# Seven quarter products for the second product of blocks 2 and 3, and a new spread of the weight preparation

## The chip, the core and the metric

The kernel runs on one core of a Trainium2 chip. The metric is the device time of one execution in microseconds. Names of engines: PE is TensorE, DVE VectorE, ACT ScalarE, POOL GpSimd, SP the engine from whose queue the DMAs are issued.

## The reference

Windowed attention over 3072 tokens of width 512 (4 sequences of 768, 8 heads of 64), and behind it two layers, each of two matrix products with a gate between them:

```python
x = attention(q, k, v, mem_k, mem_v)        # chunks of 32, softmax over 64 keys
h = x @ moe_w_in                            # 3072x512 @ 512x2048
x = (h * np.clip(h + 3.0, 0.0, 6.0) / 6.0) @ moe_w_out
h = x @ moe2_w_in
out = np.maximum(0.01 * h, h) @ moe2_w_out  # 2048x512
```

Inputs and result are fp32.

## The kernel before

The tokens are cut into six blocks of 512 columns. A matrix product at the wanted precision is made of three passes of PE: an operand is split into a high part (ACT copies it, line 341) and a low part (DVE subtracts, line 344), and PE takes high x high, low x high and high x low. The weights come from DRAM as 64-bit numbers; `decode` (lines 388 to 419) makes fp32 of them with one ACT instruction and three of DVE (lines 396 to 408).

The first layer is w1i (first product), the gate, and w1o (second product); the second layer has w2i and w2o. A product can be made plainly (`hidden`, `output`) or, for two blocks at a time, by seven products of quarter blocks in place of eight (Strassen's scheme). `seven` (line 1301) does so for first products, `second` (line 1437) for second products. For this the quarter weights, their sums and differences (a11, a12, a22, s1 to s4) are prepared by `prepare`, `joined` and `whole` (line 1208: four DVE instructions of 256 columns for each pair of weight blocks) and kept in DRAM (`kept`, `parted`); `left` (line 1255) loads a group of four quarters again when its product comes, and splits it into two parts of 1024 columns (one ACT, one DVE instruction).

The pairs of blocks have numbers: p = -2 is blocks 2 and 3, p = -1 blocks 4 and 5 of the first layer, p = 0, 1, 2 the three pairs of the second layer. Blocks 0 and 1 of the first layer are plain, with the attention of the later blocks running among them. Before the change p = -2 has its first product by `seven` and its second product plainly, block 2 and then block 3: `waiting_parts` (line 1412) splits the gated values and loads the w1o weights again, `output` (line 1027) multiplies, 12 matmuls of 512 columns for each of 16 weight blocks and each of the two blocks. p = -1 and the second layer go by sevens in both products.

What sets the order: all work is written as tasks with a key (the place in PE's sequence at which it is wanted, in units of four matmuls) and a number of buffers of each kind. `schedule` (line 103) runs a model of the engines and hands each engine its instructions in the order in which the model takes them; on the chip each engine goes through its list in that order and waits on semaphores. PE's products form one sequence, `seq2` (line 366). Preparing weights is filler: `PLAN` (lines 52 to 54) has for each of the 32 preparations a place from which it may run and a place at which it is due; before its due place it stands behind other work, from there on ahead of it. All preparation goes through DVE, ACT and SP's queue, beside the operands that PE's next products need.

Of the kernel before, what the change touches and what calls it, by code (L numbers as in the profile page):

```python
# [45 lines left out]
BOTH = 4  # L46
# [6 lines left out]
PLAN += [(290 + 9 * k, "1o", k, 320 + 9 * k) for k in range(8)]  # L53
PLAN += [(150 + 12 * k, "2i", k, 430 + 10 * k) for k in range(8)] + [(250 + 12 * k, "2o", k, 520 + 6 * k) for k in range(8)]
# [201 lines left out]
def tile_attn_moe_moe2(ctx: ExitStack, tc: tile.TileContext, raw, w1i, w1o, w2i, w2o, out):  # L256
# [41 lines left out]
    later = dram.tile([NT // (2 * N) + 1, KF // 2, 128, N], F32, name="later")  # L298
# [728 lines left out]
    def output(lay, j, f, c0, n, at=0):  # L1027
# [5 lines left out]
        if begin:  # L1033
            ybuf[lay, j] = [Buf(t) for t in ("hhyy" if j > 2 else "yyyy")]
# [248 lines left out]
    held, xs, ts1, t3s, c_of, sevens = {}, {}, {}, {}, {}, []  # L1283
# [17 lines left out]
    def seven(p, i, n):  # L1301
# [33 lines left out]
        if p < -1:  # L1335
            sevens.append(k)

        def put(r, after):
            held["b", p, i] = add(lambda e: nc.sync.dma_start(out=later[p % (PAIRED + 1), i], in_=r.t), {"SP": dma(N * 512, 330.0)}, key, after=[after], uses=[r])
# [29 lines left out]
        elif n == 7:  # L1369
            x = xs[p, i]  # L1370
            if p < -1:
                t3s[p, i] = y = Buf("w")
                done[7] = add(lambda e: nc.vector.tensor_tensor(out=half_of(y, 1), in0=bank(ba), in1=ut.t[:, 0], op=ALU.add), low, key, after=[k, done[5]], allocs=[y], uses=[ut, ba])
                c_of[p, i, "22"] = bent(lambda: y.t[:, 1], done[7], u(0), [y, ut])
                return
            done[7] = plus(lambda: x.t[:, 1], from_(ba), u(0), key, [k, done[5], c_of[p, i, "11"]], uses=[ut, ba, x])
            c_of[p, i, "22"] = bent(lambda: x.t[:, 1], done[7], u(0), [x, ut])
        elif n == 3 and p < -1:
            y = t3s[p, i]
            q = plus(lambda: y.t[:, 0], from_(bc), u(1), key, [k, done[6]], uses=[ut, bc, y])  # L1380
            c_of[p, i, "12"] = bent(lambda: y.t[:, 0], q, u(1), [y, ut])
        elif n == 4 and p < -1:
            x = xs[p, i]
            c_of[p, i, "21"] = gated(lambda: x.t[:, 1], from_(ba), [k, done[7], c_of[p, i, "11"]], lambda: x.t[:, 1], [ba, x])
# [27 lines left out]
    def waiting_parts(j, f):  # L1412

        key = pos_y["1", j, f] - 10
        src, c = (xs, t3s)[j - 2][-2, f // 2], f % 2
        z = len(quse)
        g = Buf("g" if z % OPS < 2 else "w")
        ready = [c_of[-2, f // 2, f"{c + 1}{j - 1}"]]
        hi = add(lambda e: copy(e, make(g, ([128, 2, N], F32R))[:, 0], src.t[:, c]), {"ACT": act(N)}, key, after=ready + (quse[z - OPS:z - OPS + 1] if z >= OPS else [c_of[-2, KF // 2 - 2, "22"]]), allocs=[g], uses=[src])
        lo = add(lambda e: minus(e, g.t[:, 1], src.t[:, c], g.t[:, 0].bitcast(F32)), {"DVE": dve(N)}, key, after=[hi], uses=[src, g])  # L1420
        gbuf["1", j, f, 0], gtask["1", j, f, 0] = g, (hi, lo)
        if j > 2:
            return
        w = Buf("w")
        whole_ = f >= KF // 2
        before = pos_y["1", j, f] - SOON - (3 if whole_ else 0)
        gate = max((t for t in sevens if t.key <= before), key=lambda t: t.key) if before < pos_y["1", j, 0] else ylast[j, (before - pos_y["1", j, 0]) // 3]
        k = add(lambda e: nc.sync.dma_start(out=make(w)[:, 1].bitcast(F32) if whole_ else make(w).bitcast(F32), in_=floats[f] if whole_ else halves[f]), {"SP": dma(262144 if whole_ else 524288, 360.0)}, pos_y["1", j, f] - 20, after=[gate, stored["1o", f]], allocs=[w])
        wbuf["1o", f], wtask["1o", f] = w, (k, k)
        if whole_:  # L1430
            hi = add(lambda e: copy(e, w.t[:, 0], w.t[:, 1].bitcast(F32)), {"ACT": act(512)}, key, after=[k], uses=[w])
            lo = add(lambda e: minus(e, w.t[:, 1], w.t[:, 1].bitcast(F32), w.t[:, 0].bitcast(F32)), {"DVE": dve(512)}, key, after=[hi], uses=[w])
            wtask["1o", f] = hi, lo
# [180 lines left out]
    for kind, j, f, *n in seq2:  # L1614
# [71 lines left out]
```

## Time and profile before

| | us |
|---|---|
| median of 3 runs | 1043.12 (1042.47 to 1044.17) |
| the profiled execution | 1042.63 |
| its span, first to last instruction | 1040.9 |
| PE busy | 1030.1 |
| DVE busy | 855.1 |
| ACT busy | 692.6 |

A page of the profile gives busy times and a chain that is followed back from the last instruction to what released it. PE's busy time is modelled from its pipelined matmuls, so a high share alone does not say that PE runs at its best; the distance from one matmul's start to the next does. For DVE and ACT the time shown for one instruction overlaps with the next by about 0.1 us, so what an instruction takes from the engine is read from one start to the next where instructions follow each other without a gap. The stages of the kernel follow each other in time, so busy time is read by stage.

### The profile page before, as it was taken

How to read it: one execution, taken by the hardware profiler on the slowest of the kernel's cores; microseconds unless marked ns; L12 is line 12 of the kernel's file. 1: busy time of each engine (PE TensorE's matmuls, PEld its weight loads, DVE VectorE, ACT ScalarE, POOL GpSimd, SP SyncE). 2: the span in 40 equal slices, each digit the busy share in tenths (PEclk: the TensorE clock that was granted, in tenths of full speed). 3: DMA queues.
4: the chain of work that ended last, by engine and by line, in shares of the span. 5: the costliest groups of instructions: out<-in, count | busy, mean ns of one | idle time of the engine just before them, and what ended most of it. 6: DMA issues, size and time to landing. Idle time of an engine off the chain costs nothing.

```text
span 1040.9 us, 20153 instructions
## 1 busy us (share of the span) xinstructions
PE 1030.1 (99%) x7476; PEld 849.9 (82%) x7476; DVE 855.1 (82%) x1423; ACT 692.6 (67%) x1478; POOL 22.3 (2%) x30
## 2 busy tenths in 40 slices
PE   7999999999999999999999999999999999999998
PEld 4788988888888888888888888888888888888887
DVE  6896897578999887599999898999466998566775
ACT  4896776656888554576786576775565874666753
POOL 4010000000000000000000000000000000000000
PEclk9999999999999999999999999999999999999999
DMA  9889787887897989464638894456342564522451
GB/s 266 297 241 324 258 281 238 254 293 221 286 315 232 328 280 322 157 214 135 215 129 281 268 299 151 152 170 204 128 156 81 182 200 143 179 105 99 144 182 61
DMA packets 127315, 220.50 MB, mean 212 GB/s; under 512 B 12528, under 2 KB 76016, under 8 KB 127216
## 3 DMA queue, kind: packets, MB, share of 16 engines
q1 hardware_dynamic: 127216, 219.20, 63.1%
q8 instruction: 59, 0.97, 0.4%
q14 instruction: 40, 0.33, 0.1%
HBM read 156.24 MB, written 62.91 MB: 211 GB/s over the span
## 4 chain that ended last, share of the span: by engine, by line
PE 96%; DMA 1%; DVE 1%; ACT 1%; issue 0%; SPq 0%; ACTq 0%; DVEq 0%
PE y L1322 17%; PE y L1047 15%; PE y L1490 13%; PE h L1322 11%; PE h L1490 8%; PE hx L1490 8%; PE hx L1322 8%; PE h L998 8%; PE h L1047 2%; PE at L634 2%; DMA w<-in_raw 1%; PE at L544 1%; PE at L602 1%; PE ac L461 1%; ACT w L845 0%; PE at L622 0%
## 5 line engine op out<-in xcount | busy, mean ns | idle before, releaser
L344 DVE TENSOR_TENSOR w<-w 128x512 fp32r<-128x512 f32 (+2 forms) x407 | 333.4, 858 | 28.6 <-ACT w L341 28.2
L341 ACT CAST w<-w 128x512 fp32r<-128x512 f32 (+1 forms) x296 | 226.5, 799 | 16.6 <-DMA w<-floats 7.2
L1322 PE MATMUL y<-w 128*128 128x512 f32 x516 | 124.5, 390 | 0.0
L1047 PE MATMUL y<-g,w 128*128 128x512 f32 (+1 forms) x540 | 124.4, 374 | 0.0
L1322 PEld LDWEIGHTS y<-w 128*128 128x128 f32 x516 | 96.7, 188 | 19.9
L1047 PEld LDWEIGHTS y<-g,w 128*128 128x128 f32 x540 | 94.2, 189 | 17.3
L341 ACT CAST g<-w 128x512 fp32r<-128x512 f32 x80 | 49.7, 622 | 67.6 <-PE y L1490 22.3
L1490 PE MATMUL y<-w 128*128 128x512 f32 x384 | 90.3, 389 | 0.0
L1490 PEld LDWEIGHTS y<-w 128*128 128x128 f32 x384 | 72.1, 188 | 14.9
L1296 ACT ACTIVATE w<-w 128x512 f32<-128x512 f32 x72 | 45.2, 631 | 43.0 <-DVE w L1289 21.5
L344 DVE TENSOR_TENSOR g<-w,g 128x512 fp32r<-128x512 f32 x80 | 54.8, 694 | 14.6 <-ACT g L341 14.4
L998 PE MATMUL h<-xh,w 128*128 128x512 f32 (+1 forms) x288 | 66.0, 370 | 0.0
L1490 PE MATMUL h<-w 128*128 128x512 f32 x264 | 62.1, 389 | 0.0
L1490 PE MATMUL hx<-w 128*128 128x512 f32 x252 | 59.2, 389 | 0.0
L1322 PE MATMUL h<-xl,w 128*128 128x512 f32 x240 | 58.2, 390 | 0.0
L1490 PEld LDWEIGHTS h<-w 128*128 128x128 f32 x264 | 49.6, 188 | 10.2
L998 PEld LDWEIGHTS h<-xh,w 128*128 128x128 f32 x288 | 49.7, 189 | 8.9
L1490 PEld LDWEIGHTS hx<-w 128*128 128x128 f32 x252 | 47.3, 188 | 9.8
L1322 PEld LDWEIGHTS h<-xl,w 128*128 128x128 f32 x240 | 44.9, 188 | 9.3
L1322 PE MATMUL y<-xh,w 128*128 128x512 f32 x216 | 52.0, 390 | 0.0
L1367 DVE TENSOR_TENSOR w<-y,w 128x512 f32<-128x512 f32 x35 | 24.0, 691 | 29.7 <-PE y L1322 26.9
L1322 PEld LDWEIGHTS y<-xh,w 128*128 128x128 f32 x216 | 40.5, 188 | 8.4
(243 smaller groups left out, 1836.5 us busy)
## 6 DMA issues: line engine op xcount, KB each, us to landing
w<-kept2i SPq DMA_DIRECT2D x42, 512.0 KB
w<-kept2o SPq DMA_DIRECT2D x42, 512.0 KB
w<-kept1i SPq DMA_DIRECT2D x28, 512.0 KB
a<-in_raw SPq DMA_DIRECT2D x20, 448.0 KB
w<-in_w1i SPq DMA_DIRECT2D x16, 512.0 KB
w<-in_w1o SPq DMA_DIRECT2D x16, 512.0 KB
w<-in_w2i SPq DMA_DIRECT2D x16, 512.0 KB
w<-in_w2o SPq DMA_DIRECT2D x16, 512.0 KB
```

Of the source, the lines that this page charges most:

```text
L341: nc.scalar.copy(out, in_) if e == "ACT" else engine(e).tensor_copy(out=out, in_=in_)
L344: engine(e).tensor_tensor(out=out, in0=a, in1=b, op=ALU.subtract)
L461: nc.tensor.matmul(x, ident, ident.unsqueeze(1).to_broadcast([128, c, 128]), start=True, stop=True, skip_group_check=True)
L544: nc.tensor.matmul(ps.t[h * CHUNK:(h + 1) * CHUNK, par, i * W:(i + 1) * W], qk[h // 2].t[r, gp, (h % 2) * G + c * CHUNK:(h % 2) * G + (c + ...
L602: nc.tensor.transpose(pt.t[:, i // NC, (i % NC) * 128:(i % NC + 1) * 128], pview()[:, i * 128:(i + 1) * 128], ident)
L634: nc.tensor.matmul(pv.t[(h % 2) * D:(h % 2 + 1) * D, par, (h // 2) * 2 * G + i * CHUNK:(h // 2) * 2 * G + (i + 1) * CHUNK], v[h // 2].t[r, ...
L998: nc.tensor.matmul(h.t[:, o:o + n], w.t[:, 1 if p == 1 else 0, k * 128:(k + 1) * 128], x[:, k, c0:c0 + n], start=(p == 0 and k == 0 and o ...
L1047: nc.tensor.matmul(bank(banks[d])[:, c0:c0 + n], w.t[:, 1 if p == 1 else 0, d * 128:(d + 1) * 128], g.t[:, 1 if p == 2 else 0, at:at + n], ...
L1296: return add(lambda e: nc.scalar.activation(out=at(), in_=at(), func=AF.Prelu, alpha=0.01), {"ACT": act(N)}, key, after=[after], uses=uses)
L1322: nc.tensor.matmul(bank(to), wt(l, o)[:, kt * 128:(kt + 1) * 128].bitcast(F32R), operand(p, name, 1 if q == 2 else 0, kt).bitcast(F32R), s ...
L1367: done[2] = add(lambda e: nc.vector.tensor_tensor(out=half_of(x, 0), in0=bank(bb), in1=ut.t[:, 0], op=ALU.add), low, key, after=[k, done[1 ...
L1490: nc.tensor.matmul(bank(to[d]), wt(1 if q == 1 else 0, o)[:, d * 128:(d + 1) * 128].bitcast(F32R), g.t[:, 1 if q == 2 else 0], start=(fres ...
```

## The change

Blocks 2 and 3 now have their second product by `second` too, seven products of eight steps of six matmuls; `waiting_parts` and the branches of `seven` for a plain second product go. The groups of w1o's quarters are loaded and split for p = -2 as well as for p = -1. The preparation of w1o may start at place 100 instead of 290; `joined` reads eight of w1o's blocks back from DRAM for it. The preparation of w2i may start at 305 instead of 150, that of w2o at 375 instead of 250, and their due places move by up to 12. `BOTH = 0` puts all decodes for the second layer into one chain.

The diff, cut:

```diff
-BOTH = 4
+BOTH = 0
...
-PLAN += [(290 + 9 * k, "1o", k, 320 + 9 * k) for k in range(8)]
-PLAN += [(150 + 12 * k, "2i", k, 430 + 10 * k) for k in range(8)] + [(250 + 12 * k, "2o", k, 520 + 6 * k) for k in range(8)]
+PLAN += [(100 + 1 * k, "1o", k, 100 + 13 * k) for k in range(8)]
+PLAN += [(305 + 3 * k, "2i", k, 430 + 9 * k) for k in range(8)] + [(375 + 13 * k, "2o", k, 508 + 6 * k) for k in range(8)]
...
-                if p < 0 and i == 0 and n == 1:
-                    seq2.append(("y", 0 if p < -1 else 3, KF - 1))
-        if p < -1:
-            seq2 += [("y", j, f) for j in (2, 3) for f in range(KF)][:-1]
-            continue
+                if p < -1 and i == 0 and n == 1:
+                    seq2.append(("y", 0, KF - 1))
         seq2 += [("q", p, n, i) for n in ORDER for i in range(KF // 2)]
...
+        if which == "1o" and f < KF // 2:
+            w = Buf("w")
+            k = add(lambda e: nc.sync.dma_start(out=make(w).bitcast(F32), in_=halves[f]), {"SP": dma(524288, 330.0)}, key, after=[stored[which, f], *gate], allocs=[w], late=LATE)
+            k = add(lambda e: nc.vector.tensor_tensor(out=make(m, ([128, 512], F32)), in0=w.t[:, 0].bitcast(F32), in1=w.t[:, 1].bitcast(F32), op=ALU.add), {"DVE": dve(512)}, key, after=[k], allocs=[m], uses=[w], late=LATE)
+            return m, k
...
-    def waiting_parts(j, f):
...
-            qbanks[p] = {m: [Buf(t), Buf(t)] for m, t in zip(FRESH, (("h", "hx")[p % 2], "y", "y"))} | {"m": [Buf("w"), Buf("w"), Buf("st"), Buf("st")]}
+            qbanks[p] = {m: [Buf(t), Buf(t)] for m, t in zip(FRESH, ("y", "h", "y") if p < -1 else (("h", "hx")[p % 2], "y", "y"))} | {"m": [Buf("w"), Buf("w"), Buf("st"), Buf("st")]}
...
-    prepare_before(180)
+    prepare_before(999)
...
-                x_pair(j + 1, pos_p[j + 1, 0, 1] - 18, 8)
+                x_pair(j + 1, pos_p[j + 1, 0, 1] - (18 if j > -2 else 16), 8 if j > -2 else 12)
...
-            if j > 1:
-                waiting_parts(j, f)
             output("1", j, f, 0, N)
-            if j > 1:
-                quse.append(ylast[j, f])
-            if (j, f) == (2, KF - 1):
-                prepare_before(999)
```

Two stretches of the program show the move. Line numbers are each kernel's own: `seven`'s matmuls are line 1322 before and 1324 in the changed kernel, `second`'s 1490 and 1454, the additions and the gate behind a first product 1289, 1373, 1350 and 1291, 1377, 1349, the weight preparation 396 to 408, 1189, 1208 and 393 to 405, 1186, 1210. Names: y, h and hx are PSUM banks, w and g operands in SBUF, at the attention's bank, mx its row maxima and sums, xh, xl and a the operands of a pair of blocks, wm, st and ys the weight preparation.

PE at the end of the first product of blocks 2 and 3, before:

```order
L1322 MATMUL h<-w 128x512 x12
L1047 MATMUL y<-g,w 128x512 x12
L602 MATMUL at<-ident,a 128x128 x6
L1047 MATMUL y<-g,w 128x512 x12
L634 MATMUL at<-a 64x32 x48
L1047 MATMUL y<-w 128x512 x48
L1047 MATMUL y<-g,w 128x512 x24
```

and in the changed kernel:

```order
L1324 MATMUL h<-xl,w 128x512 x12
L1324 MATMUL y<-w 128x512 x12
L1324 MATMUL h<-w 128x512 x12
L1454 MATMUL y<-g,w 128x512 x2
L599 MATMUL at<-ident,a 128x128 x6
L1454 MATMUL y<-g,w 128x512 x8
L631 MATMUL at<-a 64x32 x48
L1454 MATMUL y<-g,w 128x512 x2
L1454 MATMUL y<-w 128x512 x24
L1454 MATMUL y<-g,w 128x512 x12
```

The plain product's groups of 48 and 24 (line 1047) are gone; groups of `second` stand there, with the last attention units among them.

DVE at that place, before:

```order
L1373 TENSOR_TENSOR w<-h,w 128x512
L1189 TENSOR_TENSOR st<-w 128x512
L1289 TENSOR_TENSOR w<-y,xh 128x512
L1350 SCALAR_TENSOR_TENSOR w<-w 128x512
L1289 TENSOR_TENSOR w<-y,w 128x512
L1189 TENSOR_TENSOR st<-w 128x512
L1208 TENSOR_TENSOR ys<-st 128x256
L593 TENSOR_SCALAR mx<-mx 128x12
L594 RECIPROCAL mx<-mx 128x12
```

and in the changed kernel, beginning with the addition from bank h:

```order
L1291 TENSOR_TENSOR w<-h,w 128x512
L1210 TENSOR_TENSOR ys<-ys,wm 128x256
L344 TENSOR_TENSOR w<-w 128x1024
L1377 TENSOR_TENSOR w<-y,xh 128x512
L1210 TENSOR_TENSOR ys<-wm 128x256
L590 TENSOR_SCALAR mx<-mx 128x12
L591 RECIPROCAL mx<-mx 128x12
L1377 TENSOR_TENSOR w<-y,w 128x512
L1349 SCALAR_TENSOR_TENSOR w<-xh,w 128x512
L1349 SCALAR_TENSOR_TENSOR w<-w 128x512
```

w1o's blocks (line 1189) are no longer joined here; splits of 1024 columns and the preparation that was behind them have moved up.

DVE where the second layer begins, before, with w2o's preparation (lines 400 to 408) behind the operands:

```order
L344 TENSOR_TENSOR xl<-a,xl 128x512
L1532 SCALAR_TENSOR_TENSOR ys<-y,w 128x512 x2
L344 TENSOR_TENSOR g<-w,g 128x512 x2
L344 TENSOR_TENSOR w<-a,w 128x512
L344 TENSOR_TENSOR w<-w 128x512
L404 SCALAR_TENSOR_TENSOR wm<-w,wm 128x512
L400 TENSOR_SCALAR wm<-wm 128x512
L344 TENSOR_TENSOR w<-w 128x1024
L344 TENSOR_TENSOR w<-w 128x512
L408 SCALAR_TENSOR_TENSOR wm<-w,wm 128x512
L404 SCALAR_TENSOR_TENSOR wm<-w,wm 128x512
L408 SCALAR_TENSOR_TENSOR wm<-w,wm 128x512
```

and in the changed kernel:

```order
L344 TENSOR_TENSOR a<-a 128x512
L401 SCALAR_TENSOR_TENSOR wm<-w,wm 128x512
L397 TENSOR_SCALAR wm<-wm 128x512
L405 SCALAR_TENSOR_TENSOR wm<-w,wm 128x512
L401 SCALAR_TENSOR_TENSOR wm<-w,wm 128x512
L344 TENSOR_TENSOR xh<-w,xh 128x512
L405 SCALAR_TENSOR_TENSOR wm<-w,wm 128x512
L344 TENSOR_TENSOR a<-a,w 128x512
L344 TENSOR_TENSOR xl<-w,xl 128x512
L344 TENSOR_TENSOR xl<-a,xl 128x512
L344 TENSOR_TENSOR w<-a,w 128x512
L344 TENSOR_TENSOR w<-w 128x1024
```

Two decodes (lines 397 to 405) now stand between the operands of the second layer's first product (a, w<-a, xh, xl) and ahead of the split of 1024 columns that ends these rows.

## Rows read from the trace of the kernel before

**Rows 1.** The page's busy shares (engine, busy us, share, instructions) and its chain

```profile
PE 1030.1 (99%) x7476; PEld 849.9 (82%) x7476; DVE 855.1 (82%) x1423; ACT 692.6 (67%) x1478; POOL 22.3 (2%) x30
...
PE 96%; DMA 1%; DVE 1%; ACT 1%; issue 0%; SPq 0%; ACTq 0%; DVEq 0%
```

**Rows 2.** What PE waited for in all (us, times, longest), of seven rows

```profile
PE ac L461 <- ACT w L845: 2.0, 1, 2.0
...
PE at L602 <- DVE w L598: 1.2, 2, 0.9
```

**Rows 3.** The chain in order of time (start us, us, what), second products

```profile
504.23 10.88 PE hx L1490 x48
...
1026.47 10.89 PE h L1490 x48
```

**Rows 4.** Busy time of each engine by stage, the columns in the first line

```profile
core 0: us, PE busy (x) PEld busy (x) DVE busy (x) ACT busy (x) POOL busy (x), PEclk, DMA share, GB/s
246.80:341.00 94.20, 94.20 (x1051) 77.39 (x1051) 85.74 (x148) 77.78 (x218) 5.03 (x3) 1.00 0.82 264
341.00:424.10 83.10, 83.10 (x460) 68.87 (x459) 68.66 (x131) 40.41 (x73) 0.00 (x0) 1.00 0.88 297
424.10:504.20 80.10, 80.10 (x355) 66.42 (x354) 70.42 (x112) 53.91 (x84) 0.00 (x0) 1.00 0.55 181
504.20:580.40 76.20, 76.20 (x338) 63.17 (x337) 75.76 (x117) 52.85 (x86) 0.00 (x0) 1.00 0.61 212
580.40:656.50 76.10, 76.10 (x337) 63.07 (x337) 65.13 (x104) 52.62 (x84) 0.00 (x0) 1.00 0.66 218
656.50:732.70 76.20, 76.20 (x338) 63.17 (x337) 70.91 (x105) 52.26 (x86) 0.00 (x0) 1.00 0.53 180
```

**Rows 5.** The same view, the stretch in which DVE is full

```profile
440.00:575.00 135.00, 135.00 (x597) 111.91 (x596) 134.90 (x210) 96.23 (x152) 0.00 (x0) 1.00 0.58 195
```

**Rows 6.** DVE's instructions in order (start us, us, line, what): 1024, 512, 256 columns

```profile
513.91 1.23 DVE L344 TENSOR_TENSOR w<-w 128x1024 fp32r<-128x1024 f32 x1
515.05 0.70 DVE L344 TENSOR_TENSOR g<-w,g 128x512 fp32r<-128x512 f32 x1
515.65 0.70 DVE L344 TENSOR_TENSOR w<-w 128x512 fp32r<-128x512 f32 x1
...
519.26 1.23 DVE L344 TENSOR_TENSOR w<-w 128x1024 fp32r<-128x1024 f32 x1
...
453.54 0.43 DVE L1208 TENSOR_TENSOR ys<-st 128x256 f32<-128x256 f32 x1
453.87 0.43 DVE L1208 TENSOR_TENSOR ys<-st,ys 128x256 f32<-128x256 f32 x1
```

**Rows 7.** Groups of instructions by line (busy us, mean ns), 246.8 to 341 us

```profile
L561 DVE TENSOR_REDUCE mx<-at 128x12 f32<-128x768 f32 x4 | 3.8, 958 | 0.1
```

**Rows 8.** PE's instructions in order (start us, us, line, what) around attention units

```profile
251.47 1.17 PE L544 MATMUL at<-a 64*32 64x64 f32 x96
252.57 0.96 PE L1047 MATMUL y<-g,w 128*128 128x512 f32 x3
...
341.13 0.82 PE L602 MATMUL at<-ident,a 128*128 128x128 f32 x6
341.70 2.98 PE L1047 MATMUL y<-g,w 128*128 128x512 f32 x12
344.62 1.62 PE L634 MATMUL at<-a 64*64 64x32 f32 x96
346.17 6.19 PE L1047 MATMUL y<-w 128*128 128x512 f32 x26
```

**Rows 9.** Busy time and granted clock (PEclk) early in the trace

```profile
19.00:23.65 4.65, 2.68 (x18) 1.79 (x20) 4.22 (x12) 3.66 (x15) 2.86 (x3) 1.00 0.68 172
23.65:30.48 6.83, 6.83 (x109) 6.09 (x110) 5.41 (x10) 2.30 (x6) 2.59 (x4) 0.50 0.96 368
```

More of the change, by code (lines that the diff above doesn't have):

```diff
@@ L297, in tile_attn_moe_moe2 @@
     half = dram.tile([PLAIN, KD, 128, N], F32, name="half")
-    later = dram.tile([NT // (2 * N) + 1, KF // 2, 128, N], F32, name="later")
+    later = dram.tile([NT // (2 * N) + 2, KF // 2, 128, N], F32, name="later")
     attended = dram.tile([KD, 128, 4 * N], F32, name="attended")
@@ L1033, in output @@
         if begin:
-            ybuf[lay, j] = [Buf(t) for t in ("hhyy" if j > 2 else "yyyy")]
+            ybuf[lay, j] = [Buf(t) for t in "yyyy"]
         banks = ybuf[lay, j]
@@ L1104, in x_pair @@
         a, b = pair_of(p)
-        need = [yend["1", c] + [pk[p - 1, KF // 2 - 1, 4]] for c in (a, b)] if p >= 0 else [[*sent[a], *sent[b], *([ylast[3, 3]] if p == -1 else [])]] * 2
+        need = [yend["1", c] + [pk[p - 1, KF // 2 - 1, 4]] for c in (a, b)] if p >= 0 else [[*sent[a], *sent[b], *([pk[-2, KF // 2 - 1, 4]] if p == -1 else [])]] * 2
         homes = {"b11": "xh", "t2": "xl", "t3": "xl"} if p < -1 else {"b11": "xh", "t1": "xh", "t2": "xl", "t3": "xl"}
@@ L1281, in left @@
         return m, *ring[m]
-    held, xs, ts1, t3s, c_of, sevens = {}, {}, {}, {}, {}, []
+    held, xs, ts1, t3s, c_of = {}, {}, {}, {}, {}
     def plus(out, x, y, key, after, allocs=(), uses=()):
@@ L1334, in seven @@
         rlast[m] = [k]
-        if p < -1:
-            sevens.append(k)
         def put(r, after):
-            held["b", p, i] = add(lambda e: nc.sync.dma_start(out=later[p % (PAIRED + 1), i], in_=r.t), {"SP": dma(N * 512, 330.0)}, key, after=[after], uses=[r])
+            held["b", p, i] = add(lambda e: nc.sync.dma_start(out=later[p + 2, i], in_=r.t), {"SP": dma(N * 512, 330.0)}, key, after=[after], uses=[r])
         def u(c):
@@ L1370, in seven @@
             x = xs[p, i]
[L1371 to L1375, printed above, removed]
             done[7] = plus(lambda: x.t[:, 1], from_(ba), u(0), key, [k, done[5], c_of[p, i, "11"]], uses=[ut, ba, x])
             c_of[p, i, "22"] = bent(lambda: x.t[:, 1], done[7], u(0), [x, ut])
[L1378 to L1384, printed above, removed]
         elif n == 3:
@@ L1410, in made_as @@
         return b.t if b.t is not None else make(b, (shape, F32))
-    def waiting_parts(j, f):
[L1414 to L1433, printed above, removed]
     qbanks, quse, qops, qdone, qr = {}, [], {}, {}, {}
@@ L1454, in second @@
             r = Buf("w")
-            back = add(lambda e: nc.sync.dma_start(out=make(r, ([128, 2, N], F32)), in_=later[p % (PAIRED + 1), i:i + 2].rearrange("f p c -> p f c")), {"SP": dma(2 * N * 512, 360.0)}, pos - 20, after=[held["b", p, i], held["b", p, i + 1], *qops[p, 7, i]], allocs=[r])
+            back = add(lambda e: nc.sync.dma_start(out=make(r, ([128, 2, N], F32)), in_=later[p + 2, i:i + 2].rearrange("f p c -> p f c")), {"SP": dma(2 * N * 512, 360.0)}, pos - 20, after=[held["b", p, i], held["b", p, i + 1], *qops[p, 7, i]], allocs=[r])
             qr[p, i] = qr[p, i + 1] = r, back
@@ L1477, in second @@
         g = Buf("g" if z % OPS < 2 else "w")
-        hi = add(lambda e: copy(e, make(g, ([128, 2, N], F32R))[:, 0], src()), {"ACT": act(N)}, key, after=ready + (quse[z - OPS:z - OPS + 1] if z >= OPS else [c_of[p, KF // 2 - 1, "22"]]), allocs=[g], uses=[b])
+        hi = add(lambda e: copy(e, make(g, ([128, 2, N], F32R))[:, 0], src()), {"ACT": act(N)}, key, after=ready + (quse[z - OPS:z - OPS + 1] if z >= OPS else [c_of[p, KF // 2 - 2, "22"]]), allocs=[g], uses=[b])
         lo = add(lambda e: minus(e, g.t[:, 1], src(), g.t[:, 0].bitcast(F32)), {"DVE": dve(N)}, key, after=[hi], uses=[b, g])
@@ L1616, in tile_attn_moe_moe2 @@
             p, i, n = j, f, n[0]
-            if n == 1 and i == 0 and p == -1:
-                x_pair(p, pos_p[p, 0, 1] - 32, 12)
             seven(p, i, n)
```

## The prediction

> **What bounds the kernel now.** I read the page's busy shares and chain first, then who TensorE (PE) waits for, then the stages, then single instructions. On the page PE is busy for 1030.1 of 1040.9 us and the chain that ended last is PE for 96%; VectorE (DVE) has 82% and ScalarE (ACT) 67% [rows 1]. All that PE is shown to wait for lies in the attention and the warm-up ahead of it; no line of the two layers is in that list [rows 2]. From 504 us to the end the chain is nothing but groups of 48 matmuls in 10.88 us, 226.7 ns for each 128x512 matmul, the last group as fast as the first [rows 3]. So a matmul less is 0.2267 us less, as long as the other engines deliver.
>
> Whether they do is read by stage [rows 4]. The stages are: first product of blocks 2 and 3 (246.8 to 341), their second product, plain (to 424.1), first and second product of blocks 4 and 5 (to 504.2 and 580.4), then the second layer. DVE has 85.74 of 94.2 us, 68.66 of 83.1, 70.42 of 80.1 and 75.76 of 76.2. From 440 to 575 it is busy for 134.9 of 135 us [rows 5]: there DVE has no room, and PE is on time only because DVE had 14.4 us of room in the plain stage ahead of it. ACT has 26 us of room in 424 to 504. The average of 82% hides this.
>
> **The change, part by part.** The second product of blocks 2 and 3 was 32 steps of 12 matmuls (384); it becomes 7 x 8 steps of 6 (336). 48 matmuls x 0.2267 us = **10.88 us less on PE**. The profiled execution took 1042.63 us (span 1040.9), the median is 1043.12, so the sum stands 0.05% below the median's scale, which is nothing here. If PE stays the only limit: 1042.63 - 10.88 = 1031.75 us.
>
> What it costs is on DVE and ACT. The order of the changed kernel against the old one has on DVE 54 more instructions of 512 columns (low parts of 56 operands, the differences that seven products need and their joins, less the 40 low parts of the plain product and its weights, less 8 additions) and 12 more splits of 1024 columns (the quarter weights of w1o are now split twice, once per pair). An instruction of 512 columns holds DVE for 0.602 us, six of them from 515.65 to 519.26; one of 1024 for 1.14 (513.91 to 515.05); one of 256 for 0.33 [rows 6]. Together 54 x 0.602 + 12 x 1.14 = **46 us more on DVE**, against 10.9 us less time. ACT gets 27 more copies, 12 of them of 1024 columns, an estimate of 23 us if they take what DVE's take: I cost them at nothing; their cover is ACT's room, 42.7 us in the stage 341 to 424.1 alone [rows 4], and without it they would cost those 23. On SP's queue come 20 more DMAs, at nothing too: the DMA share is 0.88 in the plain stage, which loses its own reloads, and 0.55 to 0.61 in the two behind it [rows 4]; without that room weights would land late and PE would be seen to wait for DMAs.
>
> Where the 46 us fall decides. The weight preparation is spread anew: w1o's goes from behind the plain stage to ahead of it (it has to, its quarters are now needed 200 us earlier), w2i's goes from ahead of blocks 2 and 3 and among their first product to blocks 4 and 5, and w2o's follows it. So the stretch that was full stays full of preparation, and the stage that had 14.4 us of room gets the new operands.
>
> I price the stretch by one chain through the order, which leaves DVE no lead. It begins where DVE adds from a bank that PE has just filled (the addition from bank h that begins the changed kernel's rows of DVE in the first of the two stretches shown above; PE fills the bank 24 matmuls before the end of the first product of blocks 2 and 3), so DVE cannot be earlier there. It ends at the low part of a weight group of w2i (the last of DVE's rows in the second stretch) that PE wants for its 27th matmul of the second layer. DVE takes its rows in order. Between the two it has 321 instructions of 512 columns, 40 of 1024, 35 of 256 and 18 of 512 columns with one source, which take 0.33 as those of 256 do, and seven small ones of the attention, of which the reduction is the dear one at 0.96 us [rows 7]; an estimate of 1.4 us for the seven. 321 x 0.602 + 40 x 1.14 + 53 x 0.33 + 1.4 = 193.2 + 45.6 + 17.5 + 1.4 = **257.7 us**. PE has 24 + 3 x 336 + 27 = 1059 matmuls there, 240.0 us, and the end of two attention units: two transposes of 0.57 (341.13 to 341.70), two value products of 1.55 (344.62 to 346.17), one score product of 1.10 (251.47 to 252.57) [rows 8], 5.3 us. Together **245.3 us**. So PE must stand still for at least 257.7 - 245.3 = **12.4 us**, more than the 10.88 us it was spared. Counted the same way, the kernel before has no such chain: in its stretch 341 to 580.4 DVE has 214.8 us of work for 239.4 us [rows 4].
>
> Stage by stage the same count gives DVE 80.5 us in the new product (PE 81.5 with the attention), then 77.1 and 84.4 in the two products of blocks 4 and 5 (PE 76.2 each). So the end of the chain is where it hurts: on DVE, from 29 matmuls before the end of the second product of blocks 4 and 5 to that same group, stand 48 us of work for 39 us of PE. Weight preparation of w2i and w2o is 13.8 us of it (18 instructions at 0.33, 13 at 0.602); it is due there and goes ahead of operands that PE is about to want.
>
> On top come two terms that the chain leaves out. DVE's own waits inside it: at least as little as in 440 to 575 (0.1 in 135 us, so 0.2), at most what the stage of 246.8 to 341 loses (94.2 - 85.74 = 8.5 us). The chain's first third is of the kind of that stage, the rest of the full kind: I take 4. And the attention units, which now stand among the new product and wait behind more preparation: from 0 to 3, the list of waits having 1.2 us for two such [rows 2]; I take 1. Sum: 1042.63 - 10.88 + 12.4 + 4 + 1 = **1049.2 us**. After the chain PE is at its pace again: the same count gives DVE 77.5 and 75.4 us in the two products of the second layer's first pair, about PE's 76.2, and from there on what it was before.
>
> **Rivals.** *PE alone decides:* 1031.75 us, **faster**. For it: PE's 99%, no wait on DVE in the whole of the two layers, and 440 to 575, where a full DVE made PE wait for nothing. Against it: that is a full DVE, not an overfull one. The Trainium skill's "Perfetto Trace Analysis" (Identifying the Most-Contended Engine) says to find the engine with the highest occupancy and to optimize it first; by that the matmuls are the thing to save, and the sum would be 1031.75. The trace has DVE above PE's need in this stretch, and the same page (Optimization Strategy) allows that the most contended engine changes over time. Chance 0.07.
>
> *The chain is shorter than counted:* if DVE's waits are at their least and a part of the 256-column work overlaps, 1042.63 - 10.88 + 12.4 + 0.2 = 1044.4, about the time of before. Chance 0.10.
>
> *PE's clock falls in the new stalls:* early in the trace PE was busy 2.68 of 4.65 us up to 23.65, and then the granted clock was 0.50 (1.2 of 2.4 GHz) for 6.83 us [rows 9]. If stalls of the same size at the end of the chain bring it down once, PE does 3.4 us less in such a stretch: 1049.2 + 3.4 = 1052.6. "TensorE: Matmul & The Clock Gate" of the Trainium skill (HAM oscillation) has waits between groups of matmuls bring this about; the early rows agree, and no later row of before can show it, since PE never stops there. Chance 0.20.
>
> That the change does not do what it says is not open: the order has 4032 matmuls of 512 columns for 4080.
>
> **How the numbers follow.** The forecast, 0.63; the clock as well, 0.20; about equal, 0.10; faster, 0.07. The range begins at the floor of the chain, 1044.4, and ends with the dear ends of the two open terms and one fall of the clock: 1042.63 - 10.88 + 12.4 + 8.5 + 1 + 3.4 = 1057. A measurement can tell 0.2%, 2.1 us: faster is below 1041.0, slower above 1045.2. Faster 0.07, same 0.10, slower 0.83.
>
> **What would show it.** Right: the trace of the changed kernel has PE waiting for DVE's low parts (line 344's subtraction) for some 10 us in the 40 us around the start of the second layer, a few us more ahead of it, and DVE full from about 270 us to 640; PE's pace is 226.7 ns elsewhere. Wrong: DVE with room in that stretch (then the work was counted too high), a PE with no waits and a span near 1030, or waits that end with ACT or a DMA instead of DVE.

## The result and the profile after

The changed kernel took 1057.87 us (median of 4 runs, 1057.4 to 1058.98), the kernel before 1043.64 beside it: a ratio of 1.0128, 95% interval 1.0105 to 1.0152. It is slower, as forecast, but by 14 us and not by 6, and 0.9 us above the range. The profiled execution took 1058.05 us for a span of 1056.3, so it stands for the median.

The page's busy shares and its chain (engine, busy us, share, instructions), to be read beside [rows 1]:

```profile
PE 1025.3 (97%) x7428; PEld 839.0 (79%) x7428; DVE 897.6 (85%) x1489; ACT 710.8 (67%) x1505; POOL 22.9 (2%) x31
...
PE 77%; DVE 13%; DMA 5%; issue 3%; SPq 1%; ACT 1%; DVEq 0%; ACTq 0%
```

PE has 48 instructions less and DVE 66 more, as counted; the chain that was PE for 96% is PE for 77% and DVE for 13%. What PE waited for (us in all, times, longest); in [rows 2] no line of the two layers was named, now six of these seven are:

```profile
PE h L1324 <- DVE w L344: 5.1, 2, 5.0
PE hx L1454 <- DVE w L344: 3.4, 1, 3.4
PE y L1044 <- DVE g L344: 3.3, 1, 3.3
PE y L1454 <- DVE w L344: 2.1, 2, 1.4
PE ac L458 <- ACT w L842: 2.0, 1, 2.0
PE hx L1324 <- ACT xl L341: 1.6, 1, 1.6
...
PE y L1454 <- DVE g L344: 1.2, 2, 0.7
```

Busy time by stage, with the columns of [rows 4]. The stages are the new product (340 to 424), the two products of blocks 4 and 5 (to 508 and 588), and the two of the second layer's first pair:

```profile
246.00:340.00 94.00, 93.52 (x861) 75.53 (x860) 85.17 (x148) 71.55 (x187) 2.38 (x2) 1.00 0.91 298
340.00:424.00 84.00, 82.88 (x636) 67.52 (x635) 83.89 (x133) 61.62 (x127) 2.22 (x2) 1.00 0.76 251
424.00:508.00 84.00, 82.32 (x361) 67.21 (x360) 81.95 (x128) 59.03 (x93) 0.00 (x0) 1.00 0.58 192
508.00:588.00 80.00, 73.39 (x319) 59.15 (x318) 79.88 (x136) 51.31 (x84) 0.00 (x0) 1.00 0.81 269
588.00:664.00 76.00, 71.02 (x307) 58.30 (x306) 73.33 (x127) 53.67 (x89) 0.00 (x0) 0.98 0.85 279
664.00:740.00 76.00, 76.00 (x337) 62.72 (x336) 76.00 (x117) 54.37 (x89) 0.00 (x0) 1.00 0.60 198
```

DVE has next to no room from 340 to 588 (2.3 of 248 us), and PE stands still where it does not keep up, most of all in the 40 us ahead of 600. From 664 both are full and PE waits for nothing; the chain there is again groups of 48 matmuls in 10.88 us.

The worst of the waits, on PE (start us, us, line, what, and in brackets the idle time before it and what ended it), and what DVE did in that time:

```profile
593.34 0.61 PE L1324 MATMUL h<-xl,w 128*128 128x512 f32 x2
598.93 4.15 PE L1324 MATMUL h<-xl,w 128*128 128x512 f32 x10 [4.98 <-DVE w L344]
```

```profile
592.51 0.42 DVE L397 TENSOR_SCALAR wm<-wm 128x512 uint32<-128x512 uint32 x1
592.85 0.69 DVE L405 SCALAR_TENSOR_TENSOR wm<-w,wm 128x512 uint32<-128x512 uint32 x1
593.45 0.69 DVE L401 SCALAR_TENSOR_TENSOR wm<-w,wm 128x512 uint32<-128x512 uint32 x1
594.05 0.69 DVE L344 TENSOR_TENSOR xh<-w,xh 128x512 fp32r<-128x512 f32 x1
...
597.66 1.22 DVE L344 TENSOR_TENSOR w<-w 128x1024 fp32r<-128x1024 f32 x1
```

While PE waits, DVE decodes w2o (lines 397, 401 and 405), makes the low parts of the second layer's operands, and only then the low split of 1024 columns that PE wants: the group and the 27th matmul that the prediction named. It ends at 598.88.

**Where the time went.** The 1990th matmul from the end starts at 586.12 us in the trace before and at 598.94 in that after, 12.82 us later, although 48 matmuls (10.88 us) fewer lie ahead of it. So 23.7 us of PE's time were lost up to there, 1.9 behind it (1.7 of them by the clock, below) and 0.7 in the last stores: 23.7 + 1.9 + 0.7 - 10.88 = 15.4 = 1058.05 - 1042.63. Of the 23.7, the chain that the prediction counted makes 18.2: on DVE it ran from the addition out of bank h at 335.36 to 598.88, 263.5 us, for 245.3 us of PE's work. The other 5.5 lie ahead of it, 3.5 of them in one wait at 235 us. The last 2 are spread over the first 330 us in small pieces, and no run tells where they come from.

### The profile page after: what moved, and what is told of

It reads as the page before. It is cut to its first block, busy times and chain, and to the rows that moved or that the text cites. A ratio compares the mean times of both kernels' runs of the same rounds, so it can differ in the third digit from the quotient of the medians.

```text
span 1056.3 us, 20235 instructions
## 1 busy us (share of the span) xinstructions
PE 1025.3 (97%) x7428; PEld 839.0 (79%) x7428; DVE 897.6 (85%) x1489; ACT 710.8 (67%) x1505; POOL 22.9 (2%) x31
## 4 chain that ended last, share of the span: by engine, by line
PE 77%; DVE 13%; DMA 5%; issue 3%; SPq 1%; ACT 1%; DVEq 0%; ACTq 0%
PE y L1324 15%; PE y L1454 11%; PE h L1324 9%; PE h L1454 8%; PE h L995 8%; PE y L1044 8%; PE hx L1324 8%; DVE w L344 6%; PE hx L1454 4%; PE at L631 2%; DMA kept2i<-wm 1%; DMA w<-in_raw 1%; DVE g L344 1%; PE at L541 1%; DMA kept2i<-ys 1%
## 5 line engine op out<-in xcount | busy, mean ns | idle before, releaser
L344 DVE TENSOR_TENSOR w<-w 128x512 fp32r<-128x512 f32 (+2 forms) x453 | 365.7, 841 | 17.3 <-ACT w L341 17.2
L341 ACT CAST w<-w 128x512 fp32r<-128x512 f32 (+1 forms) x314 | 241.4, 806 | 10.2 <-DVE w L344 3.6
L1454 PE MATMUL y<-w 128*128 128x512 f32 x564 | 133.6, 390 | 2.1 <-DVE w L344 2.1
L1454 PEld LDWEIGHTS y<-w 128*128 128x128 f32 x564 | 105.5, 188 | 24.9 <-DVE w L344 2.9
L1324 PE MATMUL y<-w 128*128 128x512 f32 x516 | 124.5, 390 | 0.0
L1324 PEld LDWEIGHTS y<-w 128*128 128x128 f32 x516 | 96.6, 188 | 20.1
L1044 PE MATMUL y<-g,w 128*128 128x512 f32 (+1 forms) x432 | 96.8, 371 | 3.6 <-DVE g L344 3.3
L1044 PEld LDWEIGHTS y<-g,w 128*128 128x128 f32 x432 | 74.0, 189 | 17.3 <-DVE g L344 3.8
L1454 PE MATMUL y<-g,w 128*128 128x512 f32 x300 | 73.9, 392 | 1.2 <-DVE g L344 1.2
L1454 PE MATMUL h<-w 128*128 128x512 f32 x300 | 70.7, 389 | 0.0
L1454 PEld LDWEIGHTS y<-g,w 128*128 128x128 f32 x300 | 55.8, 188 | 14.2 <-DVE g L344 2.4
L344 DVE TENSOR_TENSOR g<-w,g 128x512 fp32r<-128x512 f32 x88 | 60.4, 693 | 7.5 <-ACT g L341 7.5
L1454 PEld LDWEIGHTS h<-w 128*128 128x128 f32 x300 | 56.2, 188 | 11.9 <-DVE w L344 0.3
L1454 PEld LDWEIGHTS hx<-w 128*128 128x128 f32 x252 | 47.2, 188 | 13.6 <-DVE w L344 3.8
```

Of the source, the lines that this page charges most:

```text
L341: nc.scalar.copy(out, in_) if e == "ACT" else engine(e).tensor_copy(out=out, in_=in_)
L344: engine(e).tensor_tensor(out=out, in0=a, in1=b, op=ALU.subtract)
L1044: nc.tensor.matmul(bank(banks[d])[:, c0:c0 + n], w.t[:, 1 if p == 1 else 0, d * 128:(d + 1) * 128], g.t[:, 1 if p == 2 else 0, at:at + n], ...
L1324: nc.tensor.matmul(bank(to), wt(l, o)[:, kt * 128:(kt + 1) * 128].bitcast(F32R), operand(p, name, 1 if q == 2 else 0, kt).bitcast(F32R), s ...
L1454: nc.tensor.matmul(bank(to[d]), wt(1 if q == 1 else 0, o)[:, d * 128:(d + 1) * 128].bitcast(F32R), g.t[:, 1 if q == 2 else 0], start=(fres ...
```

## The experiments

The theory: PE loses in each stretch between two ties (a DVE instruction that waits for PE, and a matmul that waits for a DVE instruction behind it) what DVE's work there exceeds PE's by, and the worst such stretch sets the loss. The rivals: the length of single hand-overs; late DMAs; the new operands alone; the moved preparation alone. "Excess" is DVE's work less PE's between two ties, counted through a kernel's order with the prices of the prediction. "Lost" is worked out from a trace: over all matmuls, the time to the next one's start less the median of that shape. Before, it is 47.5 us (mostly the attention and the start), after, 74.6. The length of a single wait is mostly given in this measure too; the idle time that a row shows in brackets is some 0.15 us shorter.

**1. More work inside the chain.** The sign step of w2i's decoding is done twice.

```
-            nc.vector.scalar_tensor_tensor(out=mu, in0=t.t[:, :, 1], scalar=0x80000000, in1=mu, ...)
+            for _ in range(2 if src is w2i else 1):
+                nc.vector.scalar_tensor_tensor(out=mu, in0=t.t[:, :, 1], scalar=0x80000000, in1=mu, ...)
```

> The changed kernel with the sign step of w2i's decoding done twice (the second time changes nothing): 16 more instructions of 512 columns on DVE, 14 of them inside the chain of 263.5 us that ends at 598.9 us, 2 ahead of it; the order of everything else is the same. Theory A, DVE's amount of work between the addition out of bank h and the low split of a w2i group decides, and every microsecond of it is a microsecond of PE's stall: 14 x 0.602 = 8.4 us, up to 9.6 with the two ahead, so 1057.9 + 8.4 to 9.6 = 1066.3 to 1067.5 us. Theory B, PE waits there for the length of one hand-over (bank, ACT, DVE, PE) and DVE has some room: at most 2 us, 1058 to 1060. Theory C, PE waits for weights whose DMAs are late: no change, 1058.

Measured: 1069.25 us (1066.32 to 1071.11), ratio to the kernel before 1.0222 [1.0181, 1.0262]. Its profiled execution took 1066.32, 8.3 us more than that of the changed kernel, and lost 83.0 us for 74.6: there the 8.4 us put in came out one for one, and the chain on DVE grew from 263.5 to 271.4 us. By the medians it is 11.4 us, 1.8 above the top of what was expected, so some executions lost more; what they lost it in is not shown. A hand-over's length (B, at most 1060) and late weights (C, 1058) are out as what sets the loss.

**2. Less work inside the chain.** The three DVE steps of w2i's and w2o's decoding on 64 of 512 columns.

```
+        cut = 64 if src is w2i or src is w2o else 512
-            mu = m.t.bitcast(U32)
+            mu = m.t[:, :cut].bitcast(U32)
```

> The changed kernel with the three DVE steps of w2i's and w2o's decoding done on 64 of the 512 columns, so the second layer's weights are wrong and all else, the order too, is as it was. 18 weight blocks are decoded inside the chain, at 0.33 + 2 x 0.602 us each; with an estimate of 0.1 to 0.13 for a short one that is about 21 us off DVE. Theory A: the chain falls from 263.5 to about 242 us, below PE's 245.3, so the 18.2 us of stall there go but for a few where DVE's instructions stand close together in front of PE, and the half clock after it goes too; the stall of 3.5 us at 235 us stays: 1038 to 1042 us. Theory B: the stall stays, 1055 to 1058. Theory C: 1058.

Measured: 1050.58 us (10 runs, 1048.8 to 1052.9), ratio 1.0058 [1.0038, 1.0077]. The sign was right, the size not: some 21 us of work off DVE gave back 7 and not 16 to 20. Two waits stayed around the second layer's start, of 2.4 and 2.7 us (572.7 and 588.7), and the clock fell after both; the wait at 235 us stayed too, as expected. DVE itself now stood idle for 13.6 us of the chain, for 2.3 in the changed kernel, and by the list of its waits most of that (10.5 us) was for ACT: much of what was taken off DVE went into waits for ACT. Counted with the short instructions, the whole chain has no excess left, but its last 28 us of PE's time still have 2.5 us. So the long chain was not the only one, and the last stretch had to be looked at by itself.

**3. The new places alone.** The kernel before, with w2i's and w2o's preparation where the change puts it.

```
-PLAN += [(150 + 12 * k, "2i", k, 430 + 10 * k) for k in range(8)] + [(250 + 12 * k, "2o", k, 520 + 6 * k) for k in range(8)]
+PLAN += [(305 + 3 * k, "2i", k, 430 + 9 * k) for k in range(8)] + [(375 + 13 * k, "2o", k, 508 + 6 * k) for k in range(8)]
```

> The kernel before, with its plain second product of blocks 2 and 3, and of the change only the new places of w2i's and w2o's preparation. Nothing is added to DVE; 35 us of it move from 150 to 340 us into the stretch of blocks 4 and 5. Theory A in its plain form (amount between two ties, whatever it consists of): counted through this order DVE has 13.9 us more than PE from 405 to 551 us of matmul time, and 2 to 5 us of its own waits on top: 1043.1 + 14 to 19 = 1057 to 1062 us, with the stall around the second layer's start. Rival D, it is the new operands of the seven products (46 us more on DVE) and not the moved preparation that makes the stall: 1043 to 1045.

Measured: 1060.84 us (1060.05 to 1062.14), ratio 1.0145 [1.0107, 1.0182]. Two lines of what its PE waited for, and two windows (columns as above):

```profile
PE hx L1490 <- DVE w L344: 5.0, 1, 5.0
PE h L1322 <- DVE w L344: 3.4, 1, 3.4
```

```profile
508.00:580.00 72.00, 70.08 (x302) 57.41 (x301) 71.01 (x120) 48.54 (x80) 0.00 (x0) 0.98 0.80 267
580.00:604.00 24.00, 15.35 (x56) 11.53 (x55) 24.00 (x44) 11.77 (x19) 0.00 (x0) 0.86 0.97 309
```

With no operand added, the moved preparation costs 16.5 us (1060.84 to 1044.31 beside it), at the same place and behind the same splits. Rival D is out: the new operands are not needed to make this loss.

**4. Cheaper new operands.** The 56 low parts of the new second product by a copy.

```
+        half_cost = p < -1
-        lo = add(lambda e: minus(e, g.t[:, 1], src(), g.t[:, 0].bitcast(F32)), ...)
+        lo = add(lambda e: copy(e, g.t[:, 1], g.t[:, 0].bitcast(F32)) if half_cost else minus(e, ...), ...)
```

> The changed kernel with the 56 low parts of the operands of the new second product of blocks 2 and 3 made by a copy of the high part (one source, an estimate of 0.33 us in place of 0.602), so that product is wrong and the order of all instructions is as it was. About 15 us of DVE's work go, all of it between 341 and 424 us, in the first third of the chain of 263.5 us. Theory A long (the sum over the whole chain decides, as predicted): 18.2 - 15 leaves about 3 us of stall, 1057.9 - 15 to 16.5 = 1041 to 1043 us. Theory A short (the last stretch of the chain decides by itself: counted through the order, from the additions that close the second product of blocks 4 and 5's second group to the same low split, DVE has 48.5 us of work for 38.5 us of PE, so that 10 of the 12.7 us of the whole chain's excess are made in its last 40 us): the stalls from 560 to 600 us stay, and only those at 342 to 350 and 428 us get smaller, 1054 to 1057 us. Which of the two is right also says whether the new operands or the moved preparation made the loss.

Measured: 1055.5 us (1054.21 to 1058.6), ratio 1.0121 [1.0102, 1.014], two windows of it, and below them the second one in the changed kernel:

```profile
340.00:424.00 84.00, 83.84 (x642) 68.94 (x643) 72.52 (x137) 62.52 (x129) 1.48 (x1) 1.00 0.76 263
560.00:600.00 40.00, 32.25 (x119) 24.43 (x118) 39.15 (x70) 19.79 (x33) 0.00 (x0) 0.87 0.93 307
```

```profile
560.00:600.00 40.00, 28.40 (x118) 21.53 (x117) 39.88 (x72) 19.46 (x33) 0.00 (x0) 0.99 0.95 318
```

DVE has 11.5 us of room in the new product, for 0.1 in the changed kernel, and the time falls by 2.4 us, less than the four executions differ among themselves. That room is of no use, because DVE cannot work ahead in it: by the trace it waits there 9.1 us for ACT's copies and 1.9 us for PE, and from 424 us on it is as full as before. From 560 to 600 us PE stands still for less time (it is busy 32.25 us for 28.40), but at a lower clock (0.87 for 0.99); DVE is full there in both kernels (39.15 and 39.88 us), and PE's slower matmuls take the place of waits: lost from 560 to 602 us are 13.5 for 14.8. "Short" is right: 10 of the 12.7 us of excess (12.4 in the prediction's count) are made in the last 38.5 us of PE's time, and counted again over the last 28 us it is 9.4.

**5. The old places.** The other part alone: the seven products, with the line of experiment 3 turned round (its "-" line in the changed kernel).

> The changed kernel with w2i's and w2o's preparation in the places that they had before, so the seven products of blocks 2 and 3 alone. Theory A short: counted through this order no stretch that ends at the second layer has an excess over 5 us, but one that ends in the new product does, 13.9 us between 275 and 312 us of PE's time (some 310 to 350 us in a trace), with 3.2 more ahead of it; so the stalls leave 560 to 600 us and come at 250 to 350 us, about as large: 1032.2 + 13.9 + 3.2 + 4 to 9 of DVE's own waits = 1053 to 1058 us. Rival D turned round (the moved preparation is the whole loss, the seven products cost nothing where the old places are kept): 1034 to 1040 us.

Measured: 1064.42 us (1063.45 to 1068.06), ratio 1.0208 [1.0189, 1.0228]; lost 80.8 us. Behind 376 us PE waits for nothing; the loss has left the start of the second layer for 200 to 376 us, as expected, and the time is 6 us above the top of what was expected. The row that was not foreseen, with PE's instructions in order:

```profile
356.45 1.12 PE L541 MATMUL at<-a 64*32 64x64 f32 x90 [0.17 <-ACT a L341]
367.80 1.54 PE L599 MATMUL at<-ident,a 128*128 128x128 f32 x6 [10.23 <-POOL a L595]
```

```profile
360.60:381.08 20.48, 10.87 (x116) 8.62 (x117) 18.39 (x33) 9.50 (x33) 1.56 (x1) 0.50 0.81 244
```

PE does the scores of an attention unit (line 541) until 357.57 and has nothing in its order between them and the unit's transposes (line 599), so it waits 10.2 us through the whole softmax. DVE is late by only 2.3 us of that (it takes the maximum at 359.8). The granted clock is 0.50 for 20.48 us, from within the wait on. In the changed kernel 46 matmuls (10.6 us) stand between the same two steps:

```profile
358.20 1.17 PE L541 MATMUL at<-a 64*32 64x64 f32 x96
...
369.89 0.81 PE L599 MATMUL at<-ident,a 128*128 128x128 f32 x6
```

So the order of the planner made this wait, and no count of DVE did. By an estimate from these rows the wait (10.2 us) and half of the 10.87 us that PE was busy at the half clock make 15.7 us; without them the time would be some 1049, below what the count gave. The run shows that the loss leaves the second layer's start with the old places, and that the seven products are not free there; the size that was counted it does not confirm.

**6. Two homes and an earlier start.** Pairs of w1o by turns in two sets of buffers, w2i from 261 + 9k.

```
-PLAN += [(100 + 1 * k, "1o", k, 100 + 13 * k) for k in range(8)]
+PLAN += [(100, "1o", k, 172 + 13 * k) for k in range(8)]
-PLAN += [(305 + 3 * k, "2i", k, 430 + 9 * k) ...
+PLAN += [(261 + 9 * k, "2i", k, 344 + k) ...
-            line = alone
-            parts = [joined(which, 2 * i + c, key, "st", line) for c in range(2)]
+            line = chains[1 - i % 2]
+            parts = [joined(which, 2 * i + c, key, ("st", "wm")[i % 2], line) for c in range(2)]
```

> The changed kernel with two edits to the preparation: pairs of w1o are prepared by turns in two sets of buffers (the second is idle there) so that one need not wait for the other's store, which the trace shows DVE doing ahead of the stall of 3.5 us at 235 us; and w2i's preparation starts earlier (261 + 9k, due at once). The count through the order has no excess left around 230 us and none in the last 40 us ahead of the second layer (-0.3), but 13.4 us for the stretch that ends 75 us before it. Theory A (any stretch between two ties, the worst one sets the loss): no stall at 235, the stall moves to 430 to 480 us, 13 to 16 us with DVE's waits: 1032.2 + 13.4 + 3 to 6 = 1049 to 1052 us. If only the last 40 us mattered: 1036 to 1040 us, faster than both kernels.

Measured: 1052.34 us (1051.45 to 1053.96), ratio 1.0091 [1.0075, 1.0108], 5.5 us better than the changed kernel. Windows around 235 us (the changed kernel's, then this one's), of the stretch where the count has the excess, and of the stretch ahead of the second layer:

```profile
230.00:240.00 10.00, 6.67 (x29) 5.20 (x29) 9.36 (x18) 4.95 (x10) 0.00 (x0) 1.00 0.94 306
```

```profile
230.00:240.00 10.00, 10.00 (x46) 8.29 (x45) 10.00 (x17) 6.24 (x14) 0.00 (x0) 1.00 1.03 410
424.00:508.00 84.00, 75.05 (x307) 60.42 (x306) 80.82 (x138) 52.31 (x82) 0.00 (x0) 0.92 0.71 244
508.00:588.00 80.00, 80.00 (x354) 66.27 (x353) 79.93 (x127) 54.71 (x89) 0.00 (x0) 1.00 0.65 215
```

The wait at 235 is gone, 508 to 588 us has none, and PE lost 14.6 us between 440 and 500 instead, where the count put 13.4. The two edits won 5.5 us, the wait at 235 among them; the rest of the loss they moved and did not remove.

**7. The same with light decoding.** Experiments 6 and 2 together.

> The two edits of the last experiment's kernel (two sets of buffers for w1o's preparation, w2i's preparation from 261 + 9k) and the decoding of w2i and w2o on 64 of 512 columns, so the second layer's weights are wrong: some 21 us less on DVE between 335 and 600 us. Counted through this order no stretch between two ties has an excess above 2.1 us. Theory A: the stalls from 430 to 480 us go but for 2 to 6 us of single short waits, none at 235 or 560 to 600, and the 10.88 us that PE was spared come through: 1031.75 + 2 to 6 = 1034 to 1038 us, faster than the kernel before. If the seven products cost PE something that no count of DVE shows (their operands' hand-overs, late DMAs): 1043 us or more.

Measured: 1042.99 us (10 runs, 1038.73 to 1046.34), ratio 0.9987 [0.9968, 1.0006]: no difference from the kernel before, and 5 to 9 us above what was expected. Its trace is of an execution of 1045.34, 2.3 us above the median; in it 340 to 360 us still lose 6.4 us and 440 to 480 5.7, for 1.0 and nothing before, in waits of 0.4 to 2.7 us each. So even with 21 us taken off DVE, nearly half of what the change adds, it only pays for itself: an excess near 2 us still brought some 11 us of loss, falls of the clock among it. A count of amounts is a floor; what stands above it is the order of single instructions on a full engine.

**8. GpSimd for the sums of quarter blocks.** 64 additions of 256 columns leave DVE.

```
-            ... nc.vector.tensor_tensor(out=part(name), ...), {"DVE": dve(256)}, key, ...
+            ... engine(e).tensor_tensor(out=part(name), ...), {"POOL": pool(256)} if which[0] == "2" else {"DVE": dve(256)}, key, ...
```

> The changed kernel with the four sums of quarter blocks of w2i and w2o (256 columns, 64 in all, 35 of them inside the chain) on GpSimd in place of DVE. Theory A: 35 x 0.33 = 11.6 us less in the chain, so its stall falls from 18.2 to about 7: 1057.9 - 11.6 = 1046, 1043 to 1049 with what the planner moves. Rival E, GpSimd's reading of the same memory slows DVE's instructions while it lasts (64 sums at an estimate of 0.7 us, from 1.31 us for its 512-column subtractions): DVE's own 512-column instructions get longer than 0.602 us on the mean, and half of the gain or all of it is lost, 1051 to 1058.

Measured: 1062.61 us (1061.1 to 1063.49), ratio 1.0159 [1.0121, 1.0197], 4.7 us worse than the changed kernel: rival E, and more than it gave. Two groups of the changed kernel from 335 to 664 us (line, engine, operation, tiles, shapes, count | busy us, mean ns | idle before), and the same of this one with GpSimd's:

```profile
L344 DVE TENSOR_TENSOR w<-w 128x512 fp32r<-128x512 f32 x74 | 48.6, 675 | 0.0
...
L1377 DVE TENSOR_TENSOR w<-y,w 128x512 f32<-128x512 f32 x15 | 10.2, 678 | 0.0
```

```profile
L344 DVE TENSOR_TENSOR w<-w 128x512 fp32r<-128x512 f32 x74 | 54.0, 752 | 0.0
...
L1377 DVE TENSOR_TENSOR w<-y,w 128x512 f32<-128x512 f32 x15 | 10.2, 685 | 0.2 <-PE y L1324 0.2
```

```profile
584.62 8.83 POOL L1210 TENSOR_TENSOR ys<-wm 128x256 f32<-128x256 f32 x1 [14.59 <-DMA spill<-ys]
```

DVE's subtractions of two tiles grow from 675 to 752 ns on the mean, those with one source in a bank of PE's (y) do not (678, 685); and one of GpSimd's sums, 0.73 us at its fastest, is shown for 8.83 us. "SBUF — State Buffer" of the Trainium skill (Who interferes with whom) says that a DVE instruction with two inputs in that memory contends with a GpSimd instruction that reads it; both rows agree.

Inside the chain the 11.6 us that left DVE made its work only 2.6 us shorter (258.6 us for 261.2), and its idle time grew from 2.3 to 7.3 us, which the rival had not named. The slow sums hold the buffer wm into which ACT scales the next raw block, and DVE waits for ACT, 6.4 us in two waits. The second of them, behind the sum of 8.83 us:

```profile
594.99 0.67 ACT L393 ACTIVATE wm<-w 128x512 f32<-128x512 f32 x1 [3.00 <-POOL ys L1210]
595.69 0.43 DVE L397 TENSOR_SCALAR wm<-wm 128x512 uint32<-128x512 uint32 x1 [2.84 <-ACT wm L393]
```

No version was found that beats the kernel before.

## Why the prediction was right and wrong

- **PE's 10.88 us: right.** The matmuls are fewer by 48, at the same pace wherever nothing is waited for.
- **DVE's 46 us: right in count** (66 instructions); the page's busy time grows by 897.6 - 855.1 = 42.5 us. That is another measure: an instruction by itself is busy for 0.69 us and takes 0.602 in a full row, so busy time does not test the 46.
- **ACT and SP at nothing: right but for one wait** of PE for ACT (1.6 us at 428 us); ACT has over 20 us of room in each stage, and only once did PE wait there. DVE waited 1.8 us for ACT in the chain as well, at 437 us, and ACT had itself waited 2.5 us for a store of w2i's quarters: that much the DMAs at nothing did cost.
- **The chain: right in kind, place and nearly in size.** Counted 257.7 us, measured 263.5, from the named addition to the named split. Its extra 5.8 us was the term "DVE's own waits", taken as 4, so the chain cost 18.2 us for 16.4. That 4 came near by luck, for it was taken from the room of other stages. Of the 5.8, 2.3 were idle (the wait for ACT just named, 1.8, is most of it), and 2.5 more are two instructions of 512 columns that took 1.87 and 1.96 us in place of 0.68, each while GpSimd multiplied for an attention unit. The first of them:

```profile
339.10 1.47 POOL L595 TENSOR_TENSOR a<-a,mx 128x768 f32<-128x768 f32 x1 [62.48 <-DMA kept1o<-ys]
339.25 1.87 DVE L1349 SCALAR_TENSOR_TENSOR w<-xh,w 128x512 f32<-128x512 f32 x1
```

  Every instruction of 512 columns that took over 1.2 us behind 200 us overlaps one of GpSimd, in the kernel before too. The prediction had no term for it.
- **The step that failed is the term for what lies ahead of the chain.** It was taken as 1, from 0 to 3, for attention units alone; it was 5.5, of which one wait of 3.5 us is explained. The diff moves w1o's preparation ahead of the last plain products of blocks 0 and 1, and the prediction said so, but priced DVE's work only from the first product of blocks 2 and 3 on. At 234 us DVE waits 0.64 us for a store that holds w1o's buffers and then has nine instructions, of which seven prepare w1o (joins at line 1186, sums at 1210, a low part), ahead of the low part of g that PE wants: 3.5 us. On DVE, and PE's row that ended behind it:

```profile
234.17 0.69 DVE L1186 TENSOR_TENSOR st<-w 128x512 f32<-128x512 f32 x1 [0.64 <-DMA kept1o<-st]
...
237.92 0.41 DVE L1210 TENSOR_TENSOR ys<-st,ys 128x256 f32<-128x256 f32 x1
238.26 0.68 DVE L344 TENSOR_TENSOR g<-r,g 128x512 fp32r<-128x512 f32 x1
```

```profile
238.99 0.73 PE L1044 MATMUL y<-g,w 128*128 128x512 f32 x2 [3.33 <-DVE g L344]
```

  DVE did have room shortly before (busy 9.40 of the 20 us from 200 to 220); by these rows it is the order of w1o's preparation and the operand that cost PE here, and not the amount. Experiment 6 took that store's hold away and moved w1o's due places, and the wait was gone; which of the two did it is not told. The other 2 us of the 5.5 stay open.
- **The clock: the rival came true by half,** beside the forecast and not in its place. Behind the wait of 5.0 us the granted clock was 0.50 from 599.17 to 602.58, 1.7 us of loss for the 3.4 given:

```profile
599.17:602.58 3.41, 3.41 (x9) 2.62 (x9) 3.28 (x8) 1.82 (x3) 0.00 (x0) 0.50 0.81 279
```

- **The sum:** 1042.63 - 10.88 + 18.2 + 5.5 + 1.9 + 0.7 = 1058.05. Against the forecast that is 1.8 more in the chain, 4.5 ahead of it, 1.9 behind it and 0.7 at the end. The range's upper end left the term ahead of the chain at 1; with 5.5 it would have held the measured time.
- **What would show it:** 12.4 us of waits for DVE's low parts from 560 to 600 us (some 10 were named), a few ahead, DVE full from 340 to 588 (not from 270) and again from 664. The reason was right in outline and was tested: work put into the chain came out one for one in the profiled execution (experiment 1). What the prediction didn't see is that the whole chain is not what decides, though it named the stretch: 48 us for 39 at its end are enough by themselves (experiments 3 and 4). So that 16.4 came near 18.2 does not show that the sum over the whole chain was the right sum: 15 us taken out of its first third gave back 2.4.
- **Readings of the prediction to put right:** that stretch of 39 us begins some 145 matmuls ahead of the end of the second product and not 29 (29 and 27 matmuls are 12.7 us). In the kernel before, w1o's preparation lay among the plain stage (its stores go out from 341 to 455 us) and not behind it, and its quarters are first loaded at 487 us there and at 322 in the changed kernel, 165 us earlier and not 200.
- **"PE alone decides", 1031.75:** out. Neither part of the change is free alone (experiments 3 and 5, the latter also without its one long wait, by the estimate there), and the best places that were tried left 8.9 us more than the kernel before (experiment 6).

What stays open: which of the single waits in experiment 7 come from the order that the planner wrote and which from the length of hand-overs; what experiment 5 would have taken with work between its scores and transposes, since no run has that; and the 2 us ahead of the chain.

## What to carry to other kernels

Where two engines are both near full, count the work of each between two points at which they are tied to one another, for short stretches as well as for long ones, and for every stretch that a moved step now crosses, the ones ahead of the change's own stage too. Room in a stage ahead is worth nothing if what comes next waits for another engine; the count is a floor, and on a full engine that takes its rows in order some 1 to 10 us came on top of it here, for waits and for the order of single instructions. A saving on the busiest engine, paid for with four times as much on the second, could not be had here, because the second had no room at that place.

## What the runs showed of the hardware

How a wait of PE and its clock go together was not as regular as one fall for one wait. In the changed kernel waits of 3.5 us at 235 and at 577 us left the granted clock at 1.00, and that of 5.0 us brought it down for 3.41 us. In experiment 2 the shorter wait at 572.7 us did (windows of that wait and of what followed it):

```profile
572.70:575.35 2.65, 0.40 (x3) 0.01 (x1) 2.39 (x6) 2.19 (x4) 0.00 (x0) 1.00 1.01 325
575.80:579.21 3.41, 3.41 (x10) 2.59 (x9) 3.41 (x9) 0.98 (x2) 0.00 (x0) 0.50 0.99 339
```

In experiment 6 waits of 3.9 and 4.6 us each came with 6.83 us at 0.50 that began within the wait, in experiment 5 one of 10.2 us with 20.48 us, 7.2 of them within it. A wait can so cost nearly its length again: in experiment 4 PE stood idle for 3.2 us until 576.05 and was then busy at 0.50 for 5.88 us, 2.9 of them lost. Which wait brings the clock down is not told by its length. "TensorE: Matmul & The Clock Gate" of the Trainium skill (HAM oscillation) has waits between groups of matmuls bring this about. Each of these falls came with such a wait, so the rows agree; the two waits of 3.5 us show that not every one does it.

The other surprise is GpSimd: handing it 64 small additions while it was idle made a full DVE slower (experiment 8), and even its two multiplications in the chain of the changed kernel cost DVE some 1.2 us each.
